# GpSimd's scales, low parts and integer adds of an attention and gMLP kernel, issued as two instructions of half the columns each

## The chip, the cores and the metric

The kernel runs on one NeuronCore of a Trainium2 chip. Its time is what the device takes for one execution, in microseconds; the median of three executions is 589.79 us (one of the three, at 1977.38 us, is an outlier that the median leaves out). A profile of one more execution, with every instruction of every engine, stands further down.

## What is computed

The reference is a windowed attention with linear biases, followed by a gated MLP with a spatial gate. Sizes: 8 batches, 8 heads, 576 positions, 64 numbers per head; model width 512, hidden width 1024; all in float32.

```python
scores = q @ k^T / 8 + slope[h] * -|i - j|      # kept where 0 <= i - j < 128
attn   = exp(scores - rowmax) / (rowsum + 1e-9)
x      = attn @ v                                # [8, 576, 512], heads side by side
h      = gelu_tanh(x @ w_in)                     # [8, 576, 1024]
u, v   = h[..., :512], h[..., 512:]
v_n    = (v - mean) / sqrt(var + 1e-6) * g_ln
v_s    = w_sg @ v_n + b_sg                       # mixes the 576 positions
out    = x + (u * v_s) @ w_out
```

## The kernel before

Matrix products run on TensorE in a reduced float32 format. To keep the accuracy, an operand is split into a high part (rounded to the format by ScalarE) and a low part (what the rounding left), and a product is three matmuls: high by high, high by low, low by high (`mm3`, lines 590 to 592, and the loops at lines 888 and 1039). **The low parts are subtractions, and GpSimd makes nearly all of them**: of the attention's output (`Pair.low`, line 388, 128 partitions by 576 columns), of the differences that enter the input product (line 850), of the gated hidden values (line 936 in the first batch, line 995 in the others) and of the spatial weights (lines 554 and 577). GpSimd also adds integers and subtracts low parts when the 64-bit weights are taken apart (`split64`, lines 204 and 208), scales the attention's exponentials by the inverse of their row sums (`Pair.scaled`, line 318, tiles `e` by the row `rr`), and raises variances to the power -1/2 (line 713, one column).

The attention goes in 32 pairs of heads, four for each batch. A pair's steps: scores on TensorE, minima and shifts on VectorE (lines 281, 288), exponentials on ScalarE (line 297), row sums inverted on VectorE (lines 308, 309), the scales on GpSimd (`r`, `s`, `S`), four transposes on TensorE per half (`t`, `T`, line 331), masking on VectorE (line 340), the product with the values (line 368), a gather on ScalarE and VectorE (lines 377, 380), the high part on ScalarE (line 385), the low part on GpSimd (line 388). The MLP of a batch runs beside the attention of the next. From the third batch on, its products are Strassen-like: seven block products of 12 matmuls each, whose operands are differences that VectorE forms (lines 854 and 999) and that ScalarE and GpSimd split. In a block product the first matmul reads a high part, the second the low part of the first 288 columns, and the fifth the low part of the other 288.

All steps are written down by name in one table, `ORDER`; a planner runs them in that order, and each engine issues its instructions in it. Waits between engines are put in by the tile framework, from which parts of which tiles an instruction reads and writes; so an instruction waits for the writer of its own columns. Staging buffers of the weights are loaded by SP, each once the step that read the old content is done.

The first 67 us also hold the taking apart of the weights, which VectorE, ScalarE and GpSimd share: per weight tile three operations on VectorE (lines 197, 199, 201), the integer add on GpSimd (line 204), a rounding on ScalarE and a subtraction (line 208) on VectorE or GpSimd by turns.

Of the kernel before, what the change touches and what calls it, by code (L numbers as in the profile page):

```python
# [9 lines left out]
F32 = mybir.dt.float32  # L10
# [6 lines left out]
ALU = mybir.AluOpType  # L17
# [4 lines left out]
def attention_gmlp(  # L22
# [17 lines left out]
    nc = tc.nc  # L40
# [6 lines left out]
    T = S // P  # L47
    R = S - T * P
# [29 lines left out]
    def hi_of(x):  # L78
        return x[:, 0:S]

    def lo_of(x):
        return x[:, S + R:XW]
# [43 lines left out]
    for hp in range(NPAIR):  # L126
        x = halves(f"bias{hp}", 7 * R)
# [57 lines left out]
    def split64(hi, lo, w, f, last):  # L185


        w0 = w.bitcast(U32).rearrange("p (n t) -> p n t", t=2)[:, :, 0]
        w1 = w.bitcast(I32).rearrange("p (n t) -> p n t", t=2)[:, :, 1]
        w1f = w.bitcast(F32).rearrange("p (n t) -> p n t", t=2)[:, :, 1]  # L190
        fi, ri = f.bitcast(I32), w0.bitcast(I32)

        nc.scalar.activation(ri, w0, AF.Copy, scale=2.0 ** -29)

        nc.scalar.activation(f, w1f, AF.Abs)
        yield
        nc.vector.tensor_scalar(f, f, TINY64, None, ALU.max)
        yield
        nc.vector.tensor_scalar(fi, fi, 3, 0x3FFFFFFF, ALU.logical_shift_left, ALU.bitwise_and)
        yield  # L200
        nc.vector.scalar_tensor_tensor(out=fi, in0=w1, scalar=-0x40000000, in1=fi, op0=ALU.bitwise_and, op1=ALU.bitwise_or)
        yield

        nc.gpsimd.tensor_tensor(fi, fi, ri, ALU.add)
        yield
        nc.scalar.activation(hi, f, AF.Copy)
        yield
        last.tensor_tensor(lo, f, hi.bitcast(F32), ALU.subtract)
        yield


    def burst(insts):

# [8 lines left out]
    class Pair:  # L222
# [88 lines left out]
        def scaled(self, x, y, i):  # L311
            n, m, c = x.shape
            if self.n < ON_ACT and i != T:
                for k in range(m):
                    nc.scalar.activation(x[:, k, :], y[:, k, :], AF.Copy, scale=self.rr[0:n, i + k:i + k + 1])
            else:
                k = 1 if i == 2 * T else m
                nc.gpsimd.tensor_tensor(x, y, self.rr[0:n, i:i + k].rearrange("p (m o) -> p m o", o=1).broadcast_to([n, m, c]), ALU.mult)  # L318

        def scale_first(self):  # L320
            x = self.e0.rearrange("p (m c) -> p m c", m=2)
# [63 lines left out]
            nc.scalar.copy(hi_of(xs), self.xf)  # L385

        def low(self):
            nc.gpsimd.tensor_tensor(lo_of(self.xs), self.xf, hi_of(self.xs).bitcast(F32), ALU.subtract)  # L388

        def low_tail(self):  # L390
            nc.scalar.copy(self.xs[:, S:S + R], lo_of(self.xs)[:, T * P:S].bitcast(F32))
# [22 lines left out]
    class Planner:  # L414
# [7 lines left out]
        def add(self, name, engine, length, at, run, after=(), port=False, take=(), table=None, lag=0.22):  # L422
            assert name not in self.steps, name
            self.steps[name] = (engine, length, at, run, [x for x in after if x], port or engine == "POOL", list(take), table, lag)
# [19 lines left out]
    add = plan.add  # L444
# [95 lines left out]
    def add_weights():  # L540
        for k in range(2 * NC):
            half, c = 1 - k // NC, k % NC
            hs = slice(half * F, (half + 1) * F)
            add_wide(k, WI_AT[k], (wi[:, 0, c, hs], wi[:, 1, c, hs]), w_in[c * P:(c + 1) * P, hs], lambda k=k: scratch[:, k, :], [])
        for c in range(T):
            got = {}

            def load(c=c, got=got):
                got["w"] = stage(w_sgT[c * P:(c + 1) * P, :])

            at = WS_AT + 3.0 * c
            add(f"wl{c}", "SP", 0.9, at - 8.0, load, take=[("g", [f"w-{c}"])], lag=2.0)
            add(f"wH{c}", "ACT", 0.6, at, lambda c=c, got=got: nc.scalar.activation(ws[:, 0, c, :], got["w"], AF.Copy), [f"wl{c}"])
            add(f"w-{c}", "POOL", 1.42, at, lambda c=c, got=got: nc.gpsimd.tensor_tensor(ws[:, 1, c, :], got["w"], ws[:, 0, c, :].bitcast(F32), ALU.subtract), [f"wH{c}"])
        at = WS_AT + 3.0 * T
        st = {}

        def load_tail():
            st["w"] = stage(w_sgT[T * P:S, :])
            nc.sync.dma_start(st["w"][R:2 * R], w_sgT[T * P:S, :])  # L560

        def load_bias():

            st["sb"] = mlp.tile([P, S], F32, name="wst", tag="g", bufs=NF)
            for r in range(2):
                nc.sync.dma_start(st["sb"][R + r:R + r + 1, :], b_sg.rearrange("(o t) -> o t", o=1))

        def bias_hi():
            st["sh"] = mlp.tile([P, S], F32R, name="wsh", tag="g", bufs=NF)
            nc.scalar.activation(st["sh"][R:R + 2], st["sb"][R:R + 2], AF.Copy)  # L570

        def bias_lo():
            nc.vector.scalar_tensor_tensor(out=wsB[R:R + 2], in0=st["sh"][R:R + 2].bitcast(F32), scalar=bsel[R:R + 2], in1=st["sb"][R:R + 2], op0=ALU.mult, op1=ALU.add)

        add("tl", "SP", 1.0, at - 8.0, load_tail, take=[("g", ["t-"])], lag=2.0)
        add("tH", "ACT", 0.6, at, lambda: nc.scalar.activation(wsA, st["w"], AF.Copy), ["tl"])
        add("t-", "POOL", 1.42, at, lambda: nc.gpsimd.tensor_tensor(wsB[0:R], st["w"][0:R], wsA[0:R].bitcast(F32), ALU.subtract), ["tH"])
        add("bl", "SP", 1.0, at - 8.0, load_bias, take=[("g", ["b-"])], lag=2.0)
        add("bH", "ACT", 0.68, at, bias_hi, ["bl"], take=[("g", ["b-"])])
        add("b-", "DVE", 0.98, at, bias_lo, ["bH"], port=True)  # L580
        add("gb", "SP", 0.9, LATE - 20.0, lambda: nc.sync.dma_start(gb, g_ln.rearrange("(o f) -> o f", o=1).broadcast_to([P, F])), lag=2.0)
        for c in range(NF):
            add_wide(8 + c, WO_AT + 6.0 * c, (wo[:, 0, c, :], wo[:, 1, c, :]), w_out[c * P:(c + 1) * P, :], lambda: att.tile([P, F], F32, name="tmp", tag="e", bufs=4), [("e", [f"-{8 + c}"])])
# [151 lines left out]
    def add_mlp(b):  # L735
# [95 lines left out]
        def add_fast_u(at):  # L831
# [5 lines left out]
            def u(i, j):  # L837
                return gate_u[:, 2 * i:2 * i + 2, halves[j]]
# [7 lines left out]
            def low(n):  # L846
                def run():
                    _, hi, los = slot(where[n])
                    for fs, lo in los:
                        nc.gpsimd.tensor_tensor(lo, u(*place[n])[:, fs], hi[:, fs].bitcast(F32), ALU.subtract)  # L850
                return run

            def less(n, a, c):
# [59 lines left out]
        def add_y(f, at):  # L913
# [19 lines left out]
                nc.scalar.activation(st[f"g{f}"][:, 0, :], gate_u[:, f, :], AF.Copy)  # L933

            def low():
                nc.gpsimd.tensor_tensor(st[f"g{f}"][:, 1, :], gate_u[:, f, :], st[f"g{f}"][:, 0, :].bitcast(F32), ALU.subtract)

            for i in range(2):
                need = [f"tn{b}", f"nt{b}h"] + [f"vn{b}{t}" for t in range(T)] + (["t-", "b-", "tH"] + [f"w-{c}" for c in range(T)] if b == 0 else [])
# [40 lines left out]
        def add_fast(at):  # L980
# [4 lines left out]
            def u(n):  # L985
                return gate_u[:, block[n][0], block[n][1]]
# [4 lines left out]
            def low(n, engine):  # L991
                def run():
                    _, hi, los = slot(at_slot[n])
                    for fs, lo in los:
                        engine.tensor_tensor(lo, u(n)[:, fs], hi[:, fs].bitcast(F32), ALU.subtract)  # L995
                return run

            def less(n, a, b):
# [249 lines left out]
```

## Time and profile before

| | |
|---|---|
| median of the runs | 589.79 us |
| the profiled execution's own time | 589.73 us |
| its span, from first to last instruction | 588.0 us |
| PE (TensorE matmul) busy | 563.6 us, 96% |
| DVE (VectorE) busy | 487.7 us, 83% |
| ACT (ScalarE) busy | 381.3 us, 65% |
| POOL (GpSimd) busy | 295.0 us, 50%, 288 instructions |

The profile shows start and length of every instruction on each engine. Busy time includes time in which an instruction has begun and is held up, so one and the same operation can be listed with different lengths. Matmuls are pipelined: a row of 0.30 us can follow the one ahead of it after 0.13 us, and an idle time given in front of a matmul is shorter than what the matrix engine lost there. Idle time of an engine that is not the bottleneck costs nothing.

### The profile page before, as it was taken

The page shows a single profiled execution, that of the slowest core. Times are in us where ns is not written, and L with a number is a line of the kernel's source. Part 1 is how long each engine was busy: PE and PEld are TensorE (multiplying, and loading weights), DVE is VectorE, ACT ScalarE, POOL GpSimd, SP SyncE. Part 2 cuts the span into 40 slices and gives each one's busy share as a digit, 9 for nine tenths or more (in the row PEclk, how much of TensorE's full clock was granted, in tenths as well). Part 3 has the DMA queues.
Part 4 walks back from the last instruction along what each step waited for, and adds up shares of the span by engine and source line. Part 5 has one row for each costly group of instructions (what it writes and reads, how often), then busy time and mean ns, then how long its engine had stood idle before and what let it go on. Part 6 is the DMA issues. An engine that isn't in the chain of part 4 may idle for free.

```text
span 588.0 us, 14571 instructions
## 1 busy us (share of the span) xinstructions
PE 563.6 (96%) x5495; PEld 511.6 (87%) x5495; DVE 487.7 (83%) x1336; ACT 381.3 (65%) x1066; POOL 295.0 (50%) x288
## 2 busy tenths in 40 slices
PE   6778899999999999999999999999999999999997
PEld 5556789989799889998999998988999989998996
DVE  7998999789998777899797987879897988666647
ACT  7988988474774585667775585746695666833422
POOL 3656645731246562664627643475436652475224
PEclk9989999999999999999999999999999999999999
DMA  8564233071510820654151374124532506012502
GB/s 288 199 204 122 77 120 105 23 219 57 162 72 11 284 62 1 233 173 144 59 176 42 99 238 144 68 73 139 177 120 66 187 24 188 8 33 96 168 1 80
DMA packets 43560, 69.77 MB, mean 119 GB/s; under 512 B 3554, under 2 KB 31202, under 8 KB 43492
## 3 DMA queue, kind: packets, MB, share of 16 engines
q1 hardware_dynamic: 43492, 68.86, 36.1%
q8 instruction: 43, 0.70, 0.5%
q14 instruction: 25, 0.20, 0.1%
HBM read 56.27 MB, written 12.58 MB: 117 GB/s over the span
## 4 chain that ended last, share of the span: by engine, by line
PE 82%; DVE 12%; POOL 2%; issue 2%; ACT 1%; DMA 1%; DVEq 0%; POOLq 0%; ACTq 0%
PE ps_m L590 12%; PE ps_m L1039 11%; PE ps_m L592 11%; PE ps_m L591 11%; PE ps_m L888 11%; PE ps_a L331 4%; PE ps_a L264 3%; PE ps_s L264 3%; PE ps_m L368 3%; PE ps_s L368 3%; DVE e L281 2%; DVE u L999 2%; PE ps_m L924 1%; PE ps_m L923 1%; DVE px L340 1%
## 5 line engine op out<-in xcount | busy, mean ns | idle before, releaser
L318 POOL TENSOR_TENSOR e<-e,rr 128x512 f32<-128x512 f32 (+1 forms) x88 | 76.3, 886 | 96.3 <-DVE rr L309 87.8
L297 ACT ACTIVATE e<-e,stats 128x128 f32<-128x128 f32 (+1 forms) x288 | 110.7, 387 | 19.4 <-DVE stats L281 19.0
L340 DVE TENSOR_TENSOR px<-ps_a,m_both 128x1024 f32<-128x1024 f32 x64 | 77.5, 1216 | 2.4 <-PE ps_a L331 2.2
L590 PE MATMUL ps_m<-ws,region 128*128 128x288 f32 x256 | 78.3, 306 | 0.0
L592 PE MATMUL ps_m<-ws,region 128*128 128x288 f32 x256 | 75.6, 295 | 0.0
L591 PE MATMUL ps_m<-ws,region 128*128 128x288 f32 x256 | 75.5, 295 | 0.0
L713 POOL TENSOR_TENSOR rs<-rs,mhalf 128x1 f32<-128x1 f32 (+1 forms) x40 | 30.4, 761 | 64.3 <-DVE rs L710 64.2
L388 POOL TENSOR_TENSOR xs<-xf,xs 128x576 fp32r<-128x576 f32 x32 | 47.1, 1477 | 21.6 <-ACT xs L385 21.5
L995 POOL TENSOR_TENSOR region<-u,region 128x576 fp32r<-128x576 f32 x28 | 44.1, 1580 | 21.9 <-ACT region L989 17.4
L297 ACT ACTIVATION_READ_ACCUMULATOR e<-e,stats 128x1 f32 x288 | 54.4, 189 | 0.0
L989 ACT ACTIVATE region<-u 128x576 fp32r<-128x576 f32 x35 | 23.6, 684 | 43.8 <-DVE u L999 22.1
L590 PEld LDWEIGHTS ps_m<-ws,region 128*128 128x128 f32 x256 | 48.3, 189 | 1.6 <-issue 0.6
L591 PEld LDWEIGHTS ps_m<-ws,region 128*128 128x128 f32 x256 | 48.2, 188 | 0.1
L592 PEld LDWEIGHTS ps_m<-ws,region 128*128 128x128 f32 x256 | 48.1, 188 | 0.1
L590 PE MATMUL ps_m<-wi,xs 128*128 128x512 f32 x112 | 46.4, 415 | 0.0
L592 PE MATMUL ps_m<-wi,xs 128*128 128x512 f32 x112 | 44.4, 397 | 0.7 <-POOL xs L388 0.7
L1046 DVE TENSOR_TENSOR xf<-ps_m,xf 128x576 f32<-128x576 f32 x48 | 35.9, 751 | 10.9 <-PE ps_m L1039 10.5
L591 PE MATMUL ps_m<-wi,xs 128*128 128x512 f32 x112 | 44.2, 395 | 0.0
L850 POOL TENSOR_TENSOR region<-u,region 128x576 fp32r<-128x576 f32 x18 | 27.3, 1516 | 27.3 <-ACT region L844 15.3
L331 PE MATMUL ps_a<-ident,e 128*128 128x128 f32 x256 | 38.9, 278 | 2.0 <-DVE stats L281 0.9
L929 DVE TENSOR_TENSOR u<-ps_m,u 128x576 f32<-128x576 f32 x32 | 24.0, 751 | 19.8 <-PE ps_m L924 13.4
L1039 PE MATMUL ps_m<-region,sum 128*128 128x288 f32 x252 | 36.8, 299 | 1.4 <-DVE region L995 1.1
(216 smaller groups left out, 1647.8 us busy)
## 6 DMA issues: line engine op xcount, KB each, us to landing
qk<-qkT SPq DMA_DIRECT2D x32, 576.0 KB, 4.9
sum<-store SPq DMA_DIRECT2D x36, 512.0 KB, 4.7
outT<-xf SPq DMA_DIRECT2D x31, 288.0 KB, 3.6
vt<-v_in SPq DMA_DIRECT2D x32, 256.0 KB, 4.7
wst<-w_in SPq DMA_DIRECT2D x8, 512.0 KB, 4.6
store<-sum SPq DMA_DIRECT2D x6, 512.0 KB, 5.1
vt<-v_in SPq DMA_DIRECT2D x64, 32.0 KB, 4.4
wst<-w_out SPq DMA_DIRECT2D x4, 512.0 KB, 3.6
```

What stands on the lines that cost most here:

```text
L297: nc.scalar.activation(x, x, AF.Exp, bias=self.nm[0:n, i:i + 1], scale=-1.0, accum_out=self.sm[0:n, i:i + 1])
L318: nc.gpsimd.tensor_tensor(x, y, self.rr[0:n, i:i + k].rearrange("p (m o) -> p m o", o=1).broadcast_to([n, m, c]), ALU.mult)
L331: burst([lambda t=t: nc.tensor.transpose(cv[:, t // 2, t % 2], self.pr[j][:, t, :].rearrange("p (h c) -> p h c", h=2), ident[:, j * R:j * ...
L340: nc.vector.tensor_tensor(xv, cv, mv, ALU.mult)
L388: nc.gpsimd.tensor_tensor(lo_of(self.xs), self.xf, hi_of(self.xs).bitcast(F32), ALU.subtract)
L590: nc.tensor.matmul(dst, ah, bh, start=(first and i == 0), stop=False)
L591: nc.tensor.matmul(dst, ah, bl, start=False, stop=False)
L592: nc.tensor.matmul(dst, al, bh, start=False, stop=(last and i == n - 1))
L888: nc.tensor.matmul(dst, left(n, g, c)[:, ms], right(n, h, c), start=first and c == 0 and k == 0, stop=c == 1 and k == 2, skip_group_check= ...
L995: engine.tensor_tensor(lo, u(n)[:, fs], hi[:, fs].bitcast(F32), ALU.subtract)
L1039: nc.tensor.matmul(dst, p, q, start=first and f == 0 and k == 0, stop=f == 1 and k == 2, skip_group_check=True)
L1046: nc.vector.tensor_tensor(o, st[key][:, :, 0:S2], o, ALU.add)
```

## The change

Every GpSimd operation over 512 or 576 columns becomes two instructions over 256 or 288, one right behind the other; the table of steps is the same. Not touched are the operations that were short already: the scale of the first block (128 columns), the powers (one column), and the low parts that lie in two tiles (`fifth` and `spare`, 288 columns each). Where VectorE makes a low part or a subtraction, it stays whole.

```diff
-        nc.gpsimd.tensor_tensor(fi, fi, ri, ALU.add)
+        by_halves(ALU.add, fi, fi, ri)
...
-        last.tensor_tensor(lo, f, hi.bitcast(F32), ALU.subtract)
+        if last is nc.gpsimd:
+            by_halves(ALU.subtract, lo, f, hi.bitcast(F32))
+        else:
+            last.tensor_tensor(lo, f, hi.bitcast(F32), ALU.subtract)
...
+    def by_halves(op, out, a, b, engine=None):
+
+        n = out.shape[-1] // 2
+        for cs in (slice(0, n), slice(n, 2 * n)):
+            (engine or nc.gpsimd).tensor_tensor(out[:, cs], a[:, cs], b[:, cs], op)
...
-                nc.gpsimd.tensor_tensor(x, y, self.rr[0:n, i:i + k].rearrange("p (m o) -> p m o", o=1).broadcast_to([n, m, c]), ALU.mult)
+                step = 2 if m == T else m
+                for z in range(0, m, step):
+                    nc.gpsimd.tensor_tensor(x[:, z:z + step, :], y[:, z:z + step, :], self.rr[0:n, i + z:i + z + min(k, step)].rearrange("p (m o) -> p m o", o=1).broadcast_to([n, step, c]), ALU.mult)
...
-            nc.gpsimd.tensor_tensor(lo_of(self.xs), self.xf, hi_of(self.xs).bitcast(F32), ALU.subtract)
+            by_halves(ALU.subtract, lo_of(self.xs), self.xf, hi_of(self.xs).bitcast(F32))
...
                     for fs, lo in los:
-                        engine.tensor_tensor(lo, u(n)[:, fs], hi[:, fs].bitcast(F32), ALU.subtract)
+                        for f in range(fs.start, fs.stop) if engine is nc.gpsimd else [fs]:
+                            to = lo if f is fs else lo[:, f - fs.start]
+                            engine.tensor_tensor(to, u(n)[:, f], hi[:, f].bitcast(F32), ALU.subtract)
```

The low parts at lines 554, 577, 850 and 936 are cut in the same way. The lines of the changed kernel have other numbers: most halves stand on line 219 (inside `by_halves`), the scales on 329, and the block products of line 1039 on 1053.

GpSimd in the opening, where the last low parts of the first batch's attention (`xs`), two weight subtractions (`wi`), integer adds (`tmp`) and a power (`rs`) follow each other. Before:

```order
L388 TENSOR_TENSOR xs<-xf_134,xs 128x576 [waits Activation_49] x2
L208 TENSOR_TENSOR wi<-tmp,wi 128x512 [waits Activation_49,Pool_49]
L208 TENSOR_TENSOR wi<-tmp,wi 128x512 [waits Pool_49]
L204 TENSOR_TENSOR tmp<-tmp,wst 128x512 [waits DMAHW7_49,DVE_49,PE_49]
L713 TENSOR_TENSOR rs<-rs,mhalf 128x1 [waits DVE_49]
```

The same place with the change:

```order
L219 TENSOR_TENSOR xs<-xf_134,xs 128x288 [waits Activation_49]
L219 TENSOR_TENSOR xs<-xf_134,xs 128x288
L219 TENSOR_TENSOR xs<-xf_134,xs 128x288 [waits Activation_49]
L219 TENSOR_TENSOR xs<-xf_134,xs 128x288
L219 TENSOR_TENSOR wi<-tmp,wi 128x256 [waits Activation_49,Pool_49]
L219 TENSOR_TENSOR wi<-tmp,wi 128x256 [waits Pool_49] x3
L219 TENSOR_TENSOR tmp<-tmp,wst 128x256 [waits DMAHW7_49,DVE_49,PE_49]
L219 TENSOR_TENSOR tmp<-tmp,wst 128x256
L724 TENSOR_TENSOR rs<-rs,mhalf 128x1 [waits DVE_49]
```

Each operation stands twice, in the same order; the waits for other engines are on the first half, and the second has none of its own but for GpSimd's own earlier result.

TensorE in the last block products of the last batch (`wo` are the output weights, `region` the gated values' parts). Before:

```order
L1039 MATMUL ps_m<-region,wo 128x288 [waits DVE_49,Activation_49]
L1039 MATMUL ps_m<-region,wo 128x288 [waits Pool_49]
L1039 MATMUL ps_m<-region,wo 128x288 x10
L1039 MATMUL ps_a<-region,wo 128x288 [waits Activation_49]
L1039 MATMUL ps_a<-region,wo 128x288 [waits Pool_49]
L1039 MATMUL ps_a<-region,wo 128x288 x10
```

The same place with the change:

```order
L1053 MATMUL ps_m<-region,wo 128x288 [waits DVE_49,Activation_49]
L1053 MATMUL ps_m<-region,wo 128x288 [waits Pool_49]
L1053 MATMUL ps_m<-region,wo 128x288 x2
L1053 MATMUL ps_m<-region,wo 128x288 [waits Pool_49]
L1053 MATMUL ps_m<-region,wo 128x288 x7
L1053 MATMUL ps_a<-region,wo 128x288 [waits Activation_49]
L1053 MATMUL ps_a<-region,wo 128x288 [waits Pool_49]
L1053 MATMUL ps_a<-region,wo 128x288 x2
L1053 MATMUL ps_a<-region,wo 128x288 [waits Pool_49]
L1053 MATMUL ps_a<-region,wo 128x288 x7
```

The second matmul now waits for the first half alone, and the fifth for the second half. In the same way the first of a half's four transposes waits for the first half of the scale, and the third for the second.

## Rows read from the trace of the kernel before

**Rows 1.** The page's part 4: the chain that ended last, by engine.

```profile
PE 82%; DVE 12%; POOL 2%; issue 2%; ACT 1%; DMA 1%; DVEq 0%; POOLq 0%; ACTq 0%
```

**Rows 2.** Stretches, us: length, busy of PE, PEld, DVE, ACT, POOL, clock, DMA.

```profile
15.00:67.00 52.00, 40.54 (x405) 30.52 (x406) 48.55 (x134) 44.70 (x139) 31.69 (x25) 0.97 0.47 148
67.00:588.00 521.00, 513.26 (x4996) 473.57 (x4994) 427.13 (x1141) 324.69 (x891) 257.47 (x246) 1.00 0.34 111
```

**Rows 3.** GpSimd's instructions by tile: duration ns min/median/max, first and last start.

```profile
L995 POOL TENSOR_TENSOR region<-u,region x28: 1408/1436/1957, 179.4 to 580.6; 128x576 fp32r<-128x576 f32 x28
...
L995 POOL TENSOR_TENSOR spare<-u,fifth x13: 796/810/1331, 176.9 to 567.3; 128x288 fp32r<-128x288 f32 x13
```

**Rows 4.** Groups by line and shape, GpSimd: busy us, mean ns; idle before.

```profile
L318 POOL TENSOR_TENSOR e<-e,rr 128x512 f32<-128x512 f32 x60 | 65.1, 1093 | 74.2 <-DVE rr L309 65.7 <-ACT warm L1216 8.5
...
L318 POOL TENSOR_TENSOR e<-e,rr 128x128 f32<-128x128 f32 x28 | 12.4, 443 | 22.1 <-DVE rr L309 22.1
```

**Rows 5.** Timeline of the opening, VectorE and GpSimd: start us, length us.

```profile
43.27 1.27 POOL L318 TENSOR_TENSOR e<-e,rr 128x512 f32<-128x512 f32 x1 [1.43 <-DVE rr L309]
43.56 1.27 DVE L199 TENSOR_SCALAR tmp<-tmp 128x512 int32<-128x512 int32 x1
44.51 1.48 POOL L204 TENSOR_TENSOR tmp<-tmp,wst 128x512 int32<-128x512 int32 x1
44.86 1.68 DVE L201 SCALAR_TENSOR_TENSOR tmp<-wst,tmp 128x512 int32<-128x512 int32 x1
49.78 0.43 DVE L199 TENSOR_SCALAR tmp<-tmp 128x512 int32<-128x512 int32 x1
```

**Rows 6.** The chain of waits in the opening: start us, length us, what.

```profile
15.73 1.10 DVE tmp L197
...
44.90 1.57 issue
...
51.02 1.54 issue
...
56.13 2.36 POOL wi L208 x2
58.49 1.29 POOL tmp L204
...
64.05 1.32 POOL tmp L204
```

**Rows 7.** Timeline at 393 us: two short GpSimd instructions and VectorE between.

```profile
393.21 0.81 POOL L995 TENSOR_TENSOR fifth<-u,fifth 128x288 fp32r<-128x288 f32 x1 [2.10 <-ACT fifth L989]
393.67 0.97 DVE L995 TENSOR_TENSOR region<-u,region 128x576 fp32r<-128x576 f32 x1
393.98 1.33 POOL L995 TENSOR_TENSOR spare<-u,fifth 128x288 fp32r<-128x288 f32 x1
```

**Rows 8.** Timeline of PE after 67 us: matmuls that waited, idle before.

```profile
118.92 0.40 PE L591 MATMUL ps_m<-xs,wi 128*128 128x288 f32 x1 [0.22 <-POOL xs L388]
185.88 0.40 PE L1039 MATMUL ps_m<-region,sum 128*128 128x288 f32 x1 [0.47 <-DVE region L995]
324.05 0.40 PE L1039 MATMUL ps_m<-region,sum 128*128 128x288 f32 x1 [0.21 <-DVE xf L380]
356.24 0.37 PE L888 MATMUL ps_m<-region,wi 128*128 128x288 f32 x1 [0.25 <-DVE u L897]
392.63 0.30 PE L331 MATMUL ps_a<-ident,e 128*128 128x128 f32 x1 [0.85 <-DVE stats L281]
577.94 0.40 PE L1039 MATMUL ps_m<-region,sum 128*128 128x288 f32 x1 [0.67 <-DVE region L995]
```

**Rows 9.** Timeline of VectorE ahead of the wait at 392.63 us.

```profile
388.46 3.28 DVE L999 TENSOR_TENSOR u<-u 128x576 f32<-128x576 f32 x2
```

**Rows 10.** Timeline at 125 us: a scale on GpSimd and its transposes.

```profile
125.08 1.27 POOL L318 TENSOR_TENSOR e<-e,rr 128x512 f32<-128x512 f32 x1 [6.21 <-DVE rr L309]
126.51 0.60 PE L331 MATMUL ps_a<-ident,e 128*128 128x128 f32 x4
```

More of the change, by code (lines that the diff above doesn't have):

```diff
@@ L553, in add_weights @@
             add(f"wH{c}", "ACT", 0.6, at, lambda c=c, got=got: nc.scalar.activation(ws[:, 0, c, :], got["w"], AF.Copy), [f"wl{c}"])
-            add(f"w-{c}", "POOL", 1.42, at, lambda c=c, got=got: nc.gpsimd.tensor_tensor(ws[:, 1, c, :], got["w"], ws[:, 0, c, :].bitcast(F32), ALU.subtract), [f"wH{c}"])
+            add(f"w-{c}", "POOL", 1.42, at, lambda c=c, got=got: by_halves(ALU.subtract, ws[:, 1, c, :], got["w"], ws[:, 0, c, :].bitcast(F32)), [f"wH{c}"])
         at = WS_AT + 3.0 * T
@@ L576, in add_weights @@
         add("tH", "ACT", 0.6, at, lambda: nc.scalar.activation(wsA, st["w"], AF.Copy), ["tl"])
-        add("t-", "POOL", 1.42, at, lambda: nc.gpsimd.tensor_tensor(wsB[0:R], st["w"][0:R], wsA[0:R].bitcast(F32), ALU.subtract), ["tH"])
+        add("t-", "POOL", 1.42, at, lambda: by_halves(ALU.subtract, wsB[0:R], st["w"][0:R], wsA[0:R].bitcast(F32)), ["tH"])
         add("bl", "SP", 1.0, at - 8.0, load_bias, take=[("g", ["b-"])], lag=2.0)
@@ L849, in run @@
                     for fs, lo in los:
-                        nc.gpsimd.tensor_tensor(lo, u(*place[n])[:, fs], hi[:, fs].bitcast(F32), ALU.subtract)
+                        for f in range(fs.start, fs.stop):
+                            nc.gpsimd.tensor_tensor(lo[:, f - fs.start], u(*place[n])[:, f], hi[:, f].bitcast(F32), ALU.subtract)
                 return run
@@ L935, in low @@
             def low():
-                nc.gpsimd.tensor_tensor(st[f"g{f}"][:, 1, :], gate_u[:, f, :], st[f"g{f}"][:, 0, :].bitcast(F32), ALU.subtract)
+                by_halves(ALU.subtract, st[f"g{f}"][:, 1, :], gate_u[:, f, :], st[f"g{f}"][:, 0, :].bitcast(F32))
             for i in range(2):
```

## The prediction

> **What bounds the kernel now.** I read the chain of waits first, by engine: TensorE makes up 82% of it, VectorE 12%, GpSimd 2% [rows 1]. So a longer GpSimd need not cost anything, and the question is where the other 18% lie. The table of stretches answers that [rows 2]. From 67 us to the end PE is busy for 513.3 of 521.0 us: the matrix engine is the bound, and all that any other engine could give back there is the 7.7 us in which PE idles. From 15 to 67 us it is another kernel: PE is busy for 40.5 of 52.0 us, VectorE for 48.6, ScalarE for 44.7, GpSimd for 31.7. There the chain runs along VectorE, and what is saved on it brings the whole PE-bound rest forward.
>
> Then I looked at why VectorE is that busy. Its shift on integers (L199) takes 0.43 us by itself, at 49.78 us, and 1.27 us at 43.56 us, where it meets a scale on GpSimd that runs from 43.27 to 44.54 [rows 5]. It ends 0.29 us after that scale: it was held until the scale was nearly over. The next operation (L201) begins at 44.86 and takes 1.68 us, behind an integer add that runs from 44.51 to 45.99. VectorE and GpSimd shut each other out here for nearly a whole instruction. The chain shows what that costs in the opening: at 15.73, 44.90 and 51.02 us stand 1.10, 1.57 and 1.54 us of it [rows 6], the last two as "issue", a wait for which the profile names no engine. From the first of these to the last I count seven such holds, four behind scales (L318), two behind integer adds (L204), one behind a low part (L388).
>
> The same rows show who goes first at a boundary. The add at 44.51 stands queued directly behind the scale, yet L199, which was waiting, ran before it: L199 ended at 44.83, and the add took until 45.99. The waiting engine gets the next turn.
>
> **The change part by part.** It adds 166 GpSimd instructions (60 scales, 32 low parts of line 388, 29 of line 995, 18 of line 850, 27 of weights and the first batch) and moves none; no DMA and no instruction of another engine is added.
>
> *Price of a half.* 576 columns take 1436 ns and 288 take 810, by the medians [rows 3]: two halves are 1620, so a cut costs 0.18 us. For scales, 512 columns take 1093 ns and 128 take 443 on the mean [rows 4], 1.69 ns a column, so 256 take 660 and the cut costs 0.23; these means hold disturbed runs, so I take 0.19 for all. GpSimd's busy time grows by 166 x 0.19 = 32 us from 295, half of the span still idle. The first half is ready earlier: by 0.63 us for 576 columns, by 1093 - 640 = 0.45 for a scale, by 1.29 - 0.74 = 0.55 for an integer add.
>
> *Opening.* A VectorE operation that arrives in the first half now waits for the end of that half alone, if it gets in between. All seven holds arrive there: 4 x 0.45 + 2 x 0.55 + 0.63 = 3.5 us less on the chain. Against that, four operations of GpSimd stand on the chain themselves, two L208 at 56.13, L204 at 58.49 and at 64.05 [rows 6]; each ends a cut later, 4 x 0.19 = 0.75. The net is 2.8 us. Another chain can take over before all of it is reaped: ScalarE idles for only 7.3 of these 52 us [rows 2]. Between nothing and 3.5 I take 2.0, nearer to the full sum, since the chain names VectorE's holds one by one.
>
> *Does VectorE get in between?* The kernel has such pairs already: `fifth` and `spare`, 288 columns each, one behind the other. At 393.67 us a two-input operation of VectorE arrives in the first of them, which ends at 394.02; it takes 0.97 us, and the second of the pair, begun at 393.98, takes 1.33 instead of 0.81 [rows 7, 3]. So VectorE went in between, and GpSimd's second half paid for it. The Trainium skill, in "GPSIMD Engine Reference", section 2.1 (Instruction dispatch), states that consecutive GpSimd instructions are no barrier between its cores: a core starts the next as soon as its own share is done. By that rule the seam could be closed to VectorE, and the sum would be a loss instead of a gain; the pair just read speaks against it.
>
> *After 67 us.* Six matmuls show an idle time in front that GpSimd ends, or a VectorE operation that was held: 0.22, 0.47, 0.21, 0.25, 0.85 and 0.67 us [rows 8], 2.67 together. A matmul row is 0.30 us long but follows its predecessor after 0.13, so each lost about 0.17 more than shown: 3.7 us in all. The first is a wait for a low part whose first half comes 0.63 earlier: all of its 0.39 goes. Four are behind VectorE operations held once, which gain 0.45 to 0.63 each: 0.63, 0.38, 0.42 and, of 0.84 at the last, 0.63. Ahead of 392.63 two operations are held in a row, 3.28 us for the two [rows 9]: 0.45 + 0.63 is more than the 1.02 that PE loses. That makes 3.5 us. What is late next are second halves: by 0.19, and by some 0.9 where a VectorE operation of 0.7 us goes in between. The third transpose of a half is the closest reader I found: it starts at 126.51 + 2 x 0.11 = 126.73, the scale ended at 126.35 [rows 10], a slack of 0.38 us. The cut alone is covered; a VectorE operation in between would cost 0.5. A handful of steps are that close, and VectorE does not meet most of them: I count 0.5 us. Net 3.0, between a loss of 2.5 (five such steps, no gain) and a gain of 3.7.
>
> *Sum.* Against the profiled execution's 589.73 us: 2.0 + 3.0 = 5.0 less, **584.7 us**. The median of the runs, 589.79, is the same within 0.06.
>
> **Rivals.**
> *The gain stays off the path.* VectorE is held less, but ScalarE sets the opening, and the matrix engine's waits are taken over by other steps. For it speaks ScalarE's 44.7 of 52.0 us; against it that the chain lists the holds. Only what TensorE waits for GpSimd itself would be saved, about 0.4 at 118.92 us and as much in the opening: 588.9 us.
> *The seam is closed.* GpSimd's second half starts before VectorE is let in. Then each hold gets longer by a cut: 7 x 0.19 in the opening, 6 x 0.19 after it, and 0.75 on GpSimd's own steps, less 0.4 at 118.92: 589.73 + 2.8 = 592.5. Rows 7 speak against it; in favour is only that they show one pair.
> *The second halves come late.* VectorE gets in between, and what counts is the half behind it. GpSimd's four steps on the opening's chain end up to 0.19 + 0.7 later, 3.6 us, five close transposes cost 0.5 each, 2.5, and the gains shrink to 2: 589.73 + 4.1 = 593.8. This decides wherever a half's reader has less slack than 0.9 us and VectorE is in a run of two-input operations. GpSimd's small share of the chain speaks against it; its order right behind VectorE's work in the opening speaks for it.
>
> **How the numbers follow.** Chances: 0.66 for the forecast, 0.18 for the gain off the path, 0.05 for the closed seam, 0.09 for late halves, 0.02 for something else. The forecast's own range goes from 589.73 - 3.5 - 3.7 = 582.5 to 588. The range from 581.0 to 590.3 holds it and the first rival, with a little below, since further holds on VectorE that end no wait now could matter once the rest moves; the two slower rivals are left out. Two per cent, 11.8 us, is about what a measurement of this kernel can tell from no change. More than that is above all that PE idles after 67 us, and the slower cases stay at 4: faster by over 2% 0.03, within 2% 0.94, slower by over 2% 0.03.
>
> **What would show it.** In the changed profile GpSimd should have 454 instructions and 325 to 340 us; L197, L199 and L201 in the opening should be at 0.9 us or less where they were at 1.2 to 1.7; PE's idle time from about 64 us on should fall from 7.7 to under 5, and the waits at 392 and 577 us should shrink or go. VectorE's busy time should drop by 8 to 12 us from 487.7. If holds on VectorE are as long as before, the seam is closed; if they are halved but the opening is as long as before, the gain is off the path; if new waits of PE for GpSimd turn up in front of third transposes or fifth matmuls, the halves are late.

## The result, and the profile after

**583.91 us** (median of 4 runs, 583.45 to 584.98) against 589.78 for the kernel before, a ratio of 0.990 with the interval 0.988 to 0.991. The change gains 5.9 us. That is within the 2% that the prediction called no change, but far more than the interval of the measurement leaves open. The forecast was 584.7, in a range from 581.0 to 590.3.

Everything below is read from the profiled execution of the changed kernel, 584.08 us with a span of 582.4. Its lines are some ten higher: the scale L318 is now L329, the low parts L388, L208, L554, L577 and L936 and the integer add L204 all run through one helper at L219, L995 is L1009, VectorE's L999 is L1013, L850 is L862. The page's first part, busy us by engine, and its fourth, the chain that ended last, answer to the table of before and to [rows 1]:

```profile
PE 563.5 (97%) x5495; PEld 513.5 (88%) x5495; DVE 477.2 (82%) x1336; ACT 381.5 (65%) x1066; POOL 326.6 (56%) x454
...
PE 81%; DVE 8%; ACT 5%; POOL 3%; DMA 2%; issue 1%; DVEq 0%; SPq 0%; POOLq 0%; ACTq 0%
```

GpSimd works 31.6 us more in 166 more instructions, 0.19 us each, and VectorE 10.5 us less. The rest of the answer is where VectorE was held: on the chain its share fell from 12% to 8%, and ScalarE's rose from 1% to 5%. The gain is not the clock's: the granted clock from 15 to 67 us was 0.97 before [rows 2] and is 0.97 now, and 1.00 behind it in both.

```profile
15.00:67.00 52.00, 43.11 (x440) 33.26 (x440) 48.16 (x141) 46.91 (x145) 37.55 (x49) 0.97 0.53 164
```

To split the gain between the opening and the rest, I take a point that is the same in both programs: the matmul that starts the input product of the gated half, which waits for a ScalarE operation (L823 before, L834 now). These are PE's timelines there, first of before, then of after (start us, length us, idle before it and what ended it):

```profile
66.61 0.40 PE L590 MATMUL ps_m<-xs,wi 128*128 128x288 f32 x1 [1.12 <-ACT u L823]
```

```profile
64.56 0.40 PE L601 MATMUL ps_m<-xs,wi 128*128 128x288 f32 x1 [1.24 <-ACT u L834]
```

So the opening gave 66.61 - 64.56 = 2.05 us, and the rest 521.39 - 517.84 = 3.55 of span. The tables of stretches from that point on, of before and of after (columns as in [rows 2]), show where the 3.55 lie:

```profile
66.60:588.00 521.40, 513.65 (x4996) 473.97 (x4996) 427.49 (x1142) 325.09 (x893) 257.87 (x246) 1.00 0.34 111
```

```profile
64.55:582.40 517.85, 512.29 (x4996) 474.10 (x4996) 419.10 (x1142) 325.14 (x893) 284.34 (x388) 1.00 0.34 112
```

PE's idle time fell by 2.2 us, from 7.75 to 5.56, and its busy time by 1.4 at the same number of matmuls. Part of a wait counts as busy, since a matmul is listed for 0.30 us where the next can follow after 0.13: the row ahead covers the first 0.16 us or so of a wait, and the matmul behind a wait is listed with 0.40. So part of a removed wait is taken out of the busy column. VectorE's busy time fell by 8.4.

The former wait at 392.63 us [rows 8] is gone. It stood behind two operations of VectorE that took 3.28 us together [rows 9]; this is the same pair in the changed kernel, and GpSimd beside it:

```profile
384.68 1.88 DVE L1013 TENSOR_TENSOR u<-u 128x576 f32<-128x576 f32 x2
```

```profile
383.30 1.56 POOL L1009 TENSOR_TENSOR region<-u,region 128x288 fp32r<-128x288 f32 x2
384.81 2.23 POOL L329 TENSOR_TENSOR e<-e,rr 128x256 f32<-128x256 f32 x2
```

VectorE's pair is 1.40 us shorter, and GpSimd's scale, which undisturbed is 2 x 0.61 = 1.23, takes 2.23: VectorE's second operation went in between its halves. In the opening the same happens. Where a shift of 1.27 us met a scale [rows 5], VectorE's timeline now reads

```profile
42.63 0.84 DVE L199 TENSOR_SCALAR tmp<-tmp 128x512 int32<-128x512 int32 x1
43.51 0.99 DVE L201 SCALAR_TENSOR_TENSOR tmp<-wst,tmp 128x512 int32<-128x512 int32 x1
```

0.84 and 0.99 us in place of 1.27 and 1.68.

### The profile page after: what moved, and what is told of

Its sections match the earlier page's. It is cut to its first block, busy times and chain, and to the rows that moved or that the text cites. A ratio compares the mean times of both kernels' runs of the same rounds, so it can differ in the third digit from the quotient of the medians.

```text
span 582.4 us, 14771 instructions
## 1 busy us (share of the span) xinstructions
PE 563.5 (97%) x5495; PEld 513.5 (88%) x5495; DVE 477.2 (82%) x1336; ACT 381.5 (65%) x1066; POOL 326.6 (56%) x454
## 4 chain that ended last, share of the span: by engine, by line
PE 81%; DVE 8%; ACT 5%; POOL 3%; DMA 2%; issue 1%; DVEq 0%; SPq 0%; POOLq 0%; ACTq 0%
PE ps_m L1053 13%; PE ps_m L900 12%; PE ps_m L601 11%; PE ps_m L603 11%; PE ps_m L602 11%; PE ps_a L342 4%; PE ps_a L273 3%; PE ps_m L379 3%; PE ps_s L273 3%; PE ps_s L379 3%; DVE e L290 2%; DVE px L351 2%; PE ps_m L936 1%; ACT e L306 1%; PE ps_m L935 1%
## 5 line engine op out<-in xcount | busy, mean ns | idle before, releaser
L329 POOL TENSOR_TENSOR e<-e,rr 128x256 f32<-128x256 f32 (+1 forms) x148 | 87.3, 618 | 89.2 <-DVE rr L318 75.2
L219 POOL TENSOR_TENSOR xs<-xf,xs 128x288 fp32r<-128x288 f32 x64 | 55.1, 887 | 15.4 <-ACT xs L396 15.4
L1009 POOL TENSOR_TENSOR region<-u,region 128x288 fp32r<-128x288 f32 x56 | 48.8, 896 | 13.2 <-ACT region L1001 13.2
L862 POOL TENSOR_TENSOR region<-u,region 128x288 fp32r<-128x288 f32 x36 | 31.8, 903 | 25.4 <-ACT region L855 12.6
L342 PE MATMUL ps_a<-ident,e 128*128 128x128 f32 x256 | 38.3, 277 | 0.8 <-DVE px L351 0.4
L290 DVE CUSTOM_DVE_ANT_0 e<-ps_s,bias 128x128 f32<-128x128 f32 (+1 forms) x140 | 34.9, 287 | 2.6
```

What stands on the lines that cost most here:

```text
L219: (engine or nc.gpsimd).tensor_tensor(out[:, cs], a[:, cs], b[:, cs], op)
L290: nc.vector.tensor_tensor_reduce(out=dst, in0=src, in1=bs, scale=-1.0 / math.sqrt(D), scalar=3e38, op0=ALU.add, op1=ALU.min, accum_out=acc)
L329: nc.gpsimd.tensor_tensor(x[:, z:z + step, :], y[:, z:z + step, :], self.rr[0:n, i + z:i + z + min(k, step)].rearrange("p (m o) -> p m o", ...
L342: burst([lambda t=t: nc.tensor.transpose(cv[:, t // 2, t % 2], self.pr[j][:, t, :].rearrange("p (h c) -> p h c", h=2), ident[:, j * R:j * ...
L1009: engine.tensor_tensor(to, u(n)[:, f], hi[:, f].bitcast(F32), ALU.subtract)
```

## Experiments

Each kernel ran beside the kernel before on one chip. The ratios are to the kernel before, and the change's own is 0.9897.

**The opening alone, and the rest alone.** Two kernels that share the work of the change: one cuts only the weights' operations and the first four pairs, the other only what is left.

```diff
-                step = 2 if m == T else m
+                step = 2 if m == T and self.n < ON_ACT else m
...
-            by_halves(ALU.subtract, lo_of(self.xs), self.xf, hi_of(self.xs).bitcast(F32))
+            (by_halves if self.n < ON_ACT else whole)(ALU.subtract, lo_of(self.xs), self.xf, hi_of(self.xs).bitcast(F32))
```

(and the low parts of L862, L948 and L1009 whole; the second kernel has each of these conditions turned round.) Expected of the opening alone:

> Halves only for the weights, the spatial weights and the first four pairs of heads; everything later whole, as before. Both theories agree that what is gained here is gained in the opening. Seam theory (VectorE is let in between two halves, so it is held for less): the first input-product matmul that stood at 66.6 us before and at 64.6 us with all halves stands at 64.6 again, and the time is 587.7 us (586.8 to 588.6). Early-half theory (what helps is that a reader can start after the first half): the opening gains at most the 0.7 us of one matmul, 589.1 us.

and of the rest alone:

> The complement: the weights and the first four pairs whole, halves for all the rest. Seam theory: the opening is as before (66.6 us), after it PE's waits shrink as with all halves, 586.0 us (585.2 to 587.0). The gains of this kernel and of the one with halves in the opening alone should add up to the 5.9 us of the change. Early-half theory: only waits that GpSimd itself ends go, some 0.9 us, 588.9 us.

Measured: 588.02 us, ratio 0.9968 (0.9955 to 0.998), and 585.91, ratio 0.9930 (0.9918 to 0.9942). The two parts gain 0.32% and 0.70%, together 1.02% where the change gains 1.03%: 1.9 and 4.1 us, and neither lives on the other. What the profiles were to show of the milestone did not come: it stands at 65.54 us with the opening alone and at 67.38 with the rest alone,

```profile
65.54 0.40 PE L605 MATMUL ps_m<-xs,wi 128*128 128x288 f32 x1 [1.25 <-ACT u L838]
```

```profile
67.38 0.40 PE L605 MATMUL ps_m<-xs,wi 128*128 128x288 f32 x1 [1.12 <-ACT u L838]
```

where 64.6 and 66.6 were expected. The granted clock from 15 to 67 us was 0.93 and 0.90 in these two executions, against 0.97 before and after, and each was the longest of its five; so they say little of the opening, and the split rests on the medians. With the opening alone, the wait behind VectorE's held pair is still there in PE's timeline, 0.82 us of it where before it was 0.85:

```profile
391.83 0.63 PE L346 MATMUL ps_a<-ident,e 128*128 128x128 f32 x4 [0.82 <-DVE stats L294]
```

**The other half first.** All pairs in reversed order: the half whose reader comes first is written last. If the gain came from first halves that are ready earlier, it would be gone; if it came from the seam, it would stay.

```diff
-        for cs in (slice(0, n), slice(n, 2 * n)):
+        for cs in (slice(n, 2 * n), slice(0, n)):
```

> All halves, but the second half of the columns first. Now the first reader of a result waits for the instruction that comes last, so nothing is ready earlier, and everything some 0.19 us later; the seam stays. Seam theory: VectorE's holds are as short as in the changed kernel, and most of the gain stays: 585.3 us (584.3 to 586.8). Early-half theory: the gain is gone, 589.8 us or more.

Measured: 584.72 us, ratio 0.9909 (0.9894 to 0.9924). The gain stays. By the medians the early half is worth 0.8 us at most, and the intervals overlap. The price of the wrong order shows in PE's timeline in front of a transpose, as a wait for the scale:

```profile
105.77 0.66 PE L342 MATMUL ps_a<-ident,e 128*128 128x128 f32 x4 [0.34 <-POOL e L329]
```

**As many instructions, but the seam at the end.** The second instruction has only the last 16 columns (560 of 576 and 496 of 512 go to the first), so all cuts are paid for, while an arriving VectorE operation waits as long as before.

```diff
-        n = out.shape[-1] // 2
-        for cs in (slice(0, n), slice(n, 2 * n)):
+        n = out.shape[-1]
+        for cs in (slice(0, n - 16), slice(n - 16, n)):
```

> The same 166 operations in two instructions, but the second holds only the last 16 columns. The cost of a cut (about 0.19 us for each, 32 us of GpSimd) is paid, the seam lies where the operation used to end, and nothing is ready earlier. Seam theory and early-half theory both expect no gain, and a small loss from what is later: 590.7 us (589.8 to 592.0), VectorE's busy time back at about 488 us. If the cut by itself were dear, or if a seam anywhere helped, it would be 593 us or more, or below 588 us.

Measured: 590.41 us, ratio 1.0004 (0.9992 to 1.0015). In sum nothing of the gain is left. VectorE's busy time is 485.5 us (477.2 with halves), and four of the six waits of [rows 8] are back. In PE's rows the first two answer to the second and the fourth of them; the third is a new one, for the last 16 columns of the last batch's tile `g`, which came late since VectorE took the turn in front of them:

```profile
187.20 1.07 PE L1051 MATMUL ps_m<-region,sum 128*128 128x288 f32 x6 [0.44 <-DVE region L1007]
...
357.53 0.90 PE L899 MATMUL ps_m<-region,wi 128*128 128x288 f32 x5 [0.19 <-DVE u L908]
...
577.37 0.80 PE L1051 MATMUL ps_s<-g,wo 128*128 128x288 f32 x4 [0.43 <-POOL g L1007]
```

The two largest waits, at 392.63 and 577.94 us, are not back. The transposes of the first now run through, eight of them in 1.09 us:

```profile
392.47 1.09 PE L341 MATMUL ps_a<-ident,e 128*128 128x128 f32 x8
```

VectorE came there as the long part of a low part ended, and the pair that took 3.28 us [rows 9] took 2.3. Compared matmul by matmul with the kernel before, this kernel gains 0.99 and 0.83 us at these two places and loses more than that at others, where the last columns come late. So the run shows that the cuts without an early seam give nothing in sum. That the cuts by themselves cost nothing it does not show.

**Quarters.** If a shorter instruction frees VectorE earlier, four should do more than two.

```diff
-        n = out.shape[-1] // 2
-        for cs in (slice(0, n), slice(n, 2 * n)):
+        n = out.shape[-1] // 4
+        for cs in (slice(i * n, (i + 1) * n) for i in range(4)):
...
-                step = 2 if m == T else m
+                step = 1 if m == T else m
```

> Four instructions of a quarter of the columns instead of two of a half, everywhere. Seam theory: VectorE's holds get shorter again, by at most half of what is left of them (some 14 us over its shortest times are left of 25), but PE's waits behind them are nearly all gone already, while every result of GpSimd comes another 0.38 us later and GpSimd is busy for about 390 us. So no further gain: 584.5 us (583.2 to 587.5), VectorE's busy time down to about 472 us. If GpSimd's lateness has become the limit, it is slower than the changed kernel by 3 us or more.

Measured: **603.43 us, ratio 1.0227** (1.0213 to 1.0241), 19.5 us slower than halves. The forecast of 584.5 was wrong by 18.9 us; the case that it named as the limit is what came. Its page and the stretch behind 67 us:

```profile
PE 572.9 (95%) x5495; PEld 514.9 (86%) x5495; DVE 482.4 (80%) x1336; ACT 382.3 (64%) x1066; POOL 380.5 (63%) x786
```

```profile
67.00:601.90 534.90, 521.05 (x4996) 474.70 (x4996) 424.42 (x1140) 326.16 (x894) 328.70 (x671) 1.00 0.33 108
```

GpSimd is busy for 63% of the span only, and yet PE idles 13.9 us and is busy 8.8 us more than with halves for the same 4996 matmuls: it waits, in idle time and in waits that the rows ahead cover. Three runs with quarters in one part each show where.

**Quarters in the opening only**, halves behind it:

> Quarters for the weights, the spatial weights and the first four pairs, halves for all the rest. Seam theory: in the opening the chain has left VectorE in part for ScalarE, so a shorter hold saves little there: 583.6 us (582.6 to 585.0). If VectorE's holds were still the limit of the opening, another 1 us would go, 582.9 us.

```diff
-                step = 2 if m == T else m
+                step = (1 if self.n < ON_ACT else 2) if m == T else m
```

(and four parts in the helper, but two at L948 and for later pairs). Measured: 587.17 us, ratio 0.9953 (0.9941 to 0.9965), 3.3 more than the change and outside the expected range. GpSimd is then busy for 44.69 of the 52 us from 15 to 67, and the chain of waits runs along it (start us, length us):

```profile
54.06 0.46 POOL xs L219
54.53 3.80 POOL wi L219 x8
58.32 2.11 POOL tmp L219 x4
60.44 0.53 POOL rs L724
```

With halves the last three of these rows are

```profile
52.98 3.21 POOL wi L219 x4
56.19 1.42 POOL tmp L219 x2
57.61 0.98 POOL rs L724
```

that is 1.28 us for the cuts of three operations on the chain, and a start that is 1.55 later. In this one profile the granted clock of that stretch was also lower, 0.87 against 0.97 with halves (means over pieces at 2.4 and at 1.2 GHz), so not all 3.3 can be put on GpSimd. Right in front of the milestone, from 62.0 to 66.3 us, the granted clock was 0.64 and most matmuls followed each other after 0.24 us instead of 0.13; over these matmuls the distance to the kernel with halves grew from 2.4 to 3.7 us, and 3.4 was left at the milestone. In this profile about 1 us is therefore the clock's.

**Quarters of the scales, and quarters of the low parts**, each behind the first four pairs, all else in halves:

```diff
-                step = 2 if m == T else m
+                step = (2 if self.n < ON_ACT else 1) if m == T else m
```

> The changed kernel, but the scales of the 28 pairs behind the first four in quarters of 128 columns, all else in halves. Quarters everywhere took 603.4 us, 19.5 more than halves, of which some 3 lie in the opening and 16.5 behind it. Theory 1, the transposes: PE reads a quarter each 0.11 us and GpSimd delivers one each 0.40 us, so every scale that is read as soon as it is done costs PE up to 3 x 0.30 us; with up to 56 such scales this holds most of the 16.5: 592 or more here, and PE waits for L329 in front of second, third and fourth transposes. Theory 2, the low parts: 586 or less here, and the loss is in the other kernel of this pair. Theory 3, GpSimd's busy share alone, however it comes: the scales add some 56 x 0.4 = 22 of the 54 us that GpSimd gained, so 40% of the loss, 590.5.

```diff
-            by_halves(ALU.subtract, lo_of(self.xs), self.xf, hi_of(self.xs).bitcast(F32))
+            by_halves(ALU.subtract, lo_of(self.xs), self.xf, hi_of(self.xs).bitcast(F32), parts=2 if self.n < ON_ACT else 4)
```

(likewise at L862, L948 and L1009)

> The changed kernel, but the low parts behind the first four pairs (attention, differences, gated values) in quarters of 144 columns, all else in halves, the scales too. Theory 1, the transposes wait for the scales: 588 or less here. Theory 2, the low parts' later quarters and what they hold up: 594 or more. Theory 3, GpSimd's busy share: 55% of the loss behind the opening, 593.

Measured: 588.98 us, ratio 0.9985 (0.9976 to 0.9994), and 592.99, ratio 1.0055 (1.0041 to 1.0068). Against halves the scales cost 5.1 us and the low parts 9.1; with the opening's 3.3 that is 17.4 of the 19.5. Neither the transposes alone nor the low parts alone hold it. The two losses lie nearest to the third of the theories (590.5 and 593), by which they go with GpSimd's added time (17.9 us for the scales, 24.8 for the low parts); that is a proportion and names no mechanism, and for the scales it is 1.5 us off. The places that cost are of three kinds. At a scale whose reader is close, PE goes at GpSimd's pace. With quartered scales PE's timeline and GpSimd's read

```profile
105.83 1.50 PE L342 MATMUL ps_a<-ident,e 128*128 128x128 f32 x5
```

```profile
105.82 1.12 POOL L329 TENSOR_TENSOR e<-e,rr 128x128 f32<-128x128 f32 x3
```

Four transposes of ready data take 0.60 us [rows 10]. The wait is no idle time in the table: the last three of these transposes start 0.34 to 0.36 us behind one another instead of 0.11, and as each is listed for some 0.3 us, nearly all of that counts as busy. At a low part the last quarter can come late because VectorE takes turns at the seams. This is the last batch's tile `g`, in before, after and with quartered low parts, on GpSimd:

```profile
573.93 1.43 POOL L995 TENSOR_TENSOR g<-u,g 128x576 fp32r<-128x576 f32 x1 [0.97 <-PE ps_m L1039]
```

```profile
568.71 2.14 POOL L1009 TENSOR_TENSOR g<-u,g 128x288 fp32r<-128x288 f32 x2 [0.82 <-ACT g L1001]
```

```profile
576.72 3.01 POOL L1011 TENSOR_TENSOR g<-u,g 128x144 fp32r<-128x144 f32 x4 [0.53 <-ACT g L1002]
```

and PE and VectorE beside the third of these:

```profile
579.78 0.40 PE L1055 MATMUL ps_s<-g,wo 128*128 128x288 f32 x1 [0.94 <-POOL g L1011]
```

```profile
577.56 0.84 DVE L1015 TENSOR_TENSOR u<-u 128x576 f32<-128x576 f32 x1
578.33 1.05 DVE L1011 TENSOR_TENSOR region<-u,region 128x576 fp32r<-128x576 f32 x1
```

Operations of VectorE with two inputs in the same memory as GpSimd's (L1015, L1011) run through the middle of GpSimd's four; 4 x 0.50 would be 2.0 us, 3.01 was taken, and PE stood for 0.94 us.

At a third kind of place the opposite happens: VectorE is not let in. These are VectorE and GpSimd in the run with quartered low parts, and PE at the matmul that waited at 118.92 us before [rows 8]:

```profile
110.81 2.86 DVE L643 TENSOR_TENSOR sums<-sums,wi 128x512 f32<-128x512 f32 x1
```

```profile
110.38 2.75 POOL L219 TENSOR_TENSOR xs<-xf,xs 128x144 fp32r<-128x144 f32 x6
```

```profile
118.63 0.40 PE L602 MATMUL ps_m<-xs,wi 128*128 128x288 f32 x1 [1.24 <-POOL xs L219]
```

VectorE's addition, about 0.7 us by itself, began in the first of six quarters and ended 0.54 us behind the last. Five quarters that began after it ran in front of it, 0.48 to 0.50 us each, which is their undisturbed length. What PE waits for at 118.63 comes behind this addition by way of VectorE, ScalarE and GpSimd; that wait was 0.22 us before and is 1.24 here. In the run with quarters everywhere the same addition takes 2.85 us and the same wait is 1.23. In the profiles of the kernel before and of all kernels without quarters, no GpSimd tensor operation began after a VectorE operation that was held and ended before that had its turn. With quarters everywhere this happened to seven VectorE operations, and why it does there is open.

**The scales whole, and the scales alone.** One kernel cuts all but the scales, the other the scales alone.

```diff
-                step = 2 if m == T else m
+                step = m
```

> The scales (60 of the 166 cuts) whole again, all low parts and integer adds in halves. Four of the seven holds of the opening are behind scales, and one of the two in front of the largest later wait; on the other side PE's two new waits for second halves of scales, 0.23 and 0.33 us, go. Seam theory: 585.2 us (584.2 to 586.5). If late halves of scales cost more than their seams give, it is faster than the changed kernel: 583.3 us.

```diff
-        for cs in (slice(0, n), slice(n, 2 * n)):
-            (engine or nc.gpsimd).tensor_tensor(out[:, cs], a[:, cs], b[:, cs], op)
+        (engine or nc.gpsimd).tensor_tensor(out, a, b, op)
```

> Only the scales in halves. Seam theory, as the counterpart of the run with whole scales: the gains of the two add up to about that of the change, so 588.4 us (587.4 to 589.4).

Measured: 583.87 us, ratio 0.9896 (0.9884 to 0.9909), and 588.02, ratio 0.9969 (0.9957 to 0.998). The first forecast missed: the time lies below its range, near the rival's 583.3. The second time came as forecast, but not its reason, since the two gains, 1.04% and 0.31%, do not add up to the change's 1.03%. Alone the cut scales gain 0.31%; on top of the other cuts they gain nothing. With whole scales a wait of the old kind is left in PE's timeline, behind the pair that GpSimd's whole scale holds,

```profile
387.65 0.52 PE L342 MATMUL ps_a<-ident,e 128*128 128x128 f32 x3 [0.50 <-DVE stats L290]
```

and in the changed kernel, with cut scales, groups of transposes (L342, which was L331) read

```profile
98.65 1.28 PE L342 MATMUL ps_a<-ident,e 128*128 128x128 f32 x8
...
105.68 1.43 PE L342 MATMUL ps_a<-ident,e 128*128 128x128 f32 x8
...
387.40 1.03 PE L342 MATMUL ps_a<-ident,e 128*128 128x128 f32 x8
```

In the third of these groups the cut scale frees VectorE early, and the wait of 0.50 us is not there. The first two are 0.25 and 0.40 us longer than the third: in each the seventh transpose, the first that reads the second half of its scale, starts 0.29 and 0.39 us behind the sixth instead of 0.11. Not all of that is the cut's: the two groups took 1.04 and 1.20 us in the kernel before, and 1.09 and 1.36 with whole scales. Matmul by matmul, over all 5495, the changed kernel is 0.35 us ahead of the one with whole scales at the milestone, 0.60 behind it at 106.67 us, in the second of these groups, and wins 0.6 back at the third. What is won in the opening and at the third group is given back in between.

**A version by these readings.** Scales whole, and the four operations of GpSimd that stand on the opening's chain (two subtractions, two adds, 53 to 63 us) whole too:

```diff
-        by_halves(ALU.add, fi, fi, ri)
+        by_halves(ALU.add, fi, fi, ri, parts=1 if k in (9, 10) else 2)
...
-            by_halves(ALU.subtract, lo, f, hi.bitcast(F32))
+            by_halves(ALU.subtract, lo, f, hi.bitcast(F32), parts=1 if k in (4, 6) else 2)
```

> The scales whole, and of the weights' work the two subtractions and the two integer adds that the chain of waits of the changed kernel lists behind one another on GpSimd (53 to 63 us) whole again; all else in halves. If a cut costs 0.19 us wherever GpSimd itself is the chain, the four cuts give 0.76 us back in the opening: 583.9 - 0.8 = 583.1, with the input product's first low-part matmul at about 64.1 us instead of 64.9. Rival: VectorE's operations beside these four are held longer and give it back: 583.9 or up to 584.5.

Measured: 583.32 us, ratio 0.9888 (0.9875 to 0.9901). The milestone came 0.65 us earlier than with these four cut (64.91 us with the scales whole):

```profile
64.26 0.40 PE L601 MATMUL ps_m<-xs,wi 128*128 128x288 f32 x1 [1.11 <-ACT u L834]
```

The median is 0.6 below the change's, but the intervals overlap: this is the lowest time measured, with 64 instructions fewer, and not shown to be faster than the change.

## Why the prediction was right

**The seam of halves is open: shown.** That VectorE gets in between two halves was read from one pair [rows 7]. The reversed order has nearly all of the gain, so it is not the early half; the run with the seam at the end has the same instructions, VectorE held for nearly as long as before, and in sum none of the gain. The Trainium skill, in "SBUF — State Buffer", section "Who interferes with whom", states that the port pair that VectorE and GpSimd share is an exclusive lock. [Rows 5] agree with this (0.43 us alone, 1.27 beside a scale), and the runs add that the lock is worth handing over at a finer grain, up to a point. The rival of the closed seam is out for halves: holds shrank instead of growing. The sentence "The waiting engine gets the next turn" is too wide, though: between quarters VectorE was passed over at up to five seams in a row.

**The opening: -2.0 forecast, -2.05 in the trace, 1.9 by the run with the opening alone.** The number is in part luck: 2.0 was chosen between bounds and not added up. The working behind it was only partly right. I counted 3.5 us of shorter holds, and took 2.0 because ScalarE could take over; it did, as its share of the chain (5% where it was 1%) says. But the holds did not shrink by 3.5 either. VectorE's rows for the weights, with count, busy us and mean ns, are now

```profile
L201 DVE SCALAR_TENSOR_TENSOR tmp<-wst,tmp 128x512 int32<-128x512 int32 x12 | 9.5, 790 | 0.3
L199 DVE TENSOR_SCALAR tmp<-tmp 128x512 int32<-128x512 int32 x12 | 6.5, 552 | 0.2
...
L197 DVE TENSOR_SCALAR tmp<-tmp 128x512 f32<-128x512 f32 x12 | 5.7, 473 | 0.5 <-ACT tmp L195 0.4
```

where before they were 10.3, 6.7 and 6.6 us: 1.9 less, and L199 hardly moved. Its longest hold fell from 1.27 to 0.84 us, but more of its instances are held: at 32.06 us two of them take 0.84 and 0.83, where one took 1.27 and the other 0.41 before. An operation that gets in at a seam comes to the next GpSimd instruction sooner. Of the mark "at 0.9 us or less" L197 and L199 keep to it (0.835 and 0.843), L201 does not (1.242 at the longest).

**GpSimd's own steps on the chain: +0.75 forecast, 0.65 measured** between the versions with these four cut and whole, in one profile each.

**After 67 us: -3.0 forecast, -3.55 in the trace, 4.1 by the run with the rest alone.** All six waits went, as forecast, and they are worth what the working said: compared matmul by matmul, the lead over the kernel before grows at these six by 0.37, 0.63, 0.43, 0.40, 1.02 and 0.83 us, 3.7 in all where the working had 3.5. The term for the late halves, put at 0.5, was too small. The lead is 2.04 us at the milestone and only 1.11 at 106.67 us; waits for GpSimd in front of transposes at 80.28, 99.49 and 106.67 us and, ahead of 105.30, an addition of VectorE at 102.37 that a low part's half held (1.06 us, 0.69 before) take back 0.9 before the first of the six is reached. In the last batch's `g`, five matmuls at 570.27 us take 1.16, some 0.25 more than a first of 0.40 and four that follow at 0.13 each. About as much was gained in small steps that the working did not have, 0.15 to 0.4 us each at 183, 270, 323 and 533 us of the kernel before. That the net of 3.0 came so near is partly luck. In the table of stretches 1.4 us of the 3.55 came out of busy time; the working had 1.0 for that, 0.17 for each wait.

**The marks.** 454 instructions and 326.6 us on GpSimd (325 to 340 forecast), 10.5 us less on VectorE (8 to 12), the waits at 392 and 577 us gone. PE's idle time fell to 5.56, not under 5. The mark of the late halves showed as well: waits in front of third transposes of a half at 99.49 and 106.67 us and of a fifth matmul at 570.90. PE's weight loads (PEld) list the first two, with the scale as what ended them:

```profile
99.49 0.20 PEld L342 LDWEIGHTS ps_a<-ident,e 128*128 128x128 f32 x2 [0.26 <-POOL e L329]
...
106.67 0.20 PEld L342 LDWEIGHTS ps_a<-ident,e 128*128 128x128 f32 x2 [0.35 <-POOL e L329]
```

**The rivals.** The gain is on the path, against the first. The late halves were the mechanism with the right place and a wrong point: for halves they take back some 1.2 us, and with quarters late results, and VectorE passed over at seams, take back all of the gain and 13.4 us more. The forecast that quarters would be no worse than halves was drawn from the seam alone, and fell by this.

**The range.** Its lower end, 582.5, took 3.5 us for the opening without the 0.75 that the working had just subtracted; with it the end is 583.2, and the time lies within either. The upper end of 588 has no sum behind it: the worst cases of the two terms would give 592.2. And the two per cent that a measurement was said to need are too many, since the intervals here are 0.1 to 0.15% to either side.

**What is left open.** Why VectorE is passed over between some quarters is not shown. How the scales' gains and losses cancel was read from one profile of each kernel. Of the opening's 3.3 us with quarters, about 1 stood under the lower clock in the one profile; whether quarters bring that clock about is not known. The opening's own share of the gain has no second profile at the same clock.

## What to carry to other kernels

Where GpSimd has time to spare and VectorE is seen at two or three times its own length beside GpSimd's instructions, cut GpSimd's long instructions in two: the cut costs 0.19 us on an engine that idles, and the longest shifts of VectorE in the opening went from 1.27 to 0.84 us. Do not go on cutting: each seam also lets VectorE delay what remains of GpSimd's operation, and once its readers are closer than that, the loss is larger than the gain; and between quarters VectorE was not always let in. Look for these effects in the length of operations and of groups of matmuls, since little of them shows up as idle time, and leave whole what is itself on the chain.

## What the runs showed of the hardware

Between whole instructions and between halves, the turn went to the VectorE operation that waited wherever these traces show one; between quarters it did not always, and one operation of about 0.7 us took 2.86. Where VectorE does get its turns, GpSimd pays for them: the same work on `g` took it 1.43 us as one instruction, 2.14 as two and 3.01 as four. The cost of one more instruction is about the same at every length, by the medians: 1436 ns for 576 columns [rows 3], 812 for 288, 496 for 144, so 0.19 and 0.18 us a cut; and in the run with the short tail, 16 columns took as little as 0.21 us:

```profile
L1007 POOL TENSOR_TENSOR region<-u,region x56: 212/1064/1926, 180.8 to 582.7; 128x560 fp32r<-128x560 f32 x28, 128x16 fp32r<-128x16 f32 x28
```

And an engine at 63% of the span cost a kernel 2.3%: its share of busy time did not tell how near its readers were.
